# Attention over long keys on one core: VectorE, ScalarE and TensorE programs turned into one-block loops

## The chip, the cores and the metric

The kernel runs on one core of one Trainium2 chip. The metric is the device time of that core in microseconds (us), lower is better.

## The reference

```python
B, H, Sq, Skv, Dh = 8, 16, 16, 2048, 256          # bfloat16 throughout
scale = q.shape[-1] ** -0.5
scores = jnp.einsum('bhqd,bhkd->bhqk', q, k) * scale
attn = softmax(scores, axis=-1)
return jnp.einsum('bhqk,bhkd->bhqd', attn, v)
```

There are 128 heads with 16 queries each. K and V are 128 MB each (in units of 2^20 bytes) and are read once, so about 269 million bytes must come from HBM. Eight heads make a block; there are 16 blocks, each with 8 MB of K and 8 MB of V.

## The kernel before

Each engine has a list of jobs. A job counts up a semaphore when it is done, and later jobs wait for its value. The lists are written out as straight programs, except for TensorE, whose blocks 1 to 14 are one loop.

By a fetch this document means one instruction packet in the trace's DMA records. In the span of the kernel before there are ten: four of 16 KB on queue 8 and six of 8 KB on queue 14. Queue 8's are put down to TensorE. Queue 14's are put down to VectorE, ScalarE and SyncE: with VectorE and ScalarE straight again it carried seven in place of two. By a fetch block we mean the instructions that one such packet holds. How many those are is an estimate: three of queue 14's packets begin after the 57th, 186th and 316th instruction of VectorE in the trace, 129 and 130 apart, so about 130 for 8 KB and 260 for 16 KB. `head_slot` is the program's request at which slot of such a block a loop's first instruction is placed.

## Time and profile before

| what | value |
|---|---|
| time, median | 640.6 us (three runs); 640.75 with those made beside the changed kernel |
| span of the profile | 639.2 us |
| busy: PE, VectorE, ScalarE | 77%, 67%, 16% |
| packet time of all 16 DMA engines, mean of one | 635.1 us |
| granted clock (share of the full TensorE clock) | 0.936 |

First the page of the kernel before: busy time by engine, the 40 slices of the span (a digit is the busy tenth of a slice), and the DMA queues (packets, MB, share of 16 engines).

```profile
span 639.2 us, 4824 instructions
PE 489.1 (77%) x2176; PEld 166.7 (26%) x1680; DVE 427.8 (67%) x372; ACT 99.1 (16%) x208; POOL 4.2 (1%) x7
...
DMA  9999999999999999999999999999999999999996
GB/s 322 428 431 426 432 433 441 435 427 428 421 438 429 431 429 429 437 439 425 437 414 443 431 429 431 425 430 433 437 441 425 432 417 440 429 429 430 421 427 258
...
q1 hardware_dynamic: 13488, 269.51, 98.7%
q10 hardware_dynamic: 2288, 1.03, 0.6%
q8 instruction: 4, 0.07, 0.0%
q14 instruction: 6, 0.05, 0.0%
```

The DMA engines are busy from end to end. The two last lines look like nothing: ten packets of instructions that take 0.0% of the DMA engines.

The chain of waits of the kernel before, in its steady part and at its end (start, length, what):

```profile
429.19 8.90 DVE KB L126 x4
438.09 0.02 issue
438.11 30.14 DMA KN<-in_k_dram
468.25 0.02 issue
468.27 8.90 DVE KB L126 x4
...
556.30 30.15 DMA KN<-in_k_dram
586.45 0.02 issue
...
608.24 28.35 PE O_ps L177 x256
636.59 0.02 issue
636.61 0.48 DVE O_fin L323
```

The first K half of a block lands every 39.08 us, 30 us after its issue. Its own 4 MB take 9.7 us at 431 GB/s; the rest is the queue of loads ahead of it. VectorE and TensorE therefore have slack in the steady part: VectorE waited 139.3 us in all for K loads, TensorE 22.2 us for V loads. At the end TensorE works through 256 matmuls without a gap (28.35 us, with fetches at 617.8 and 631.9 us in it), but its last ones are released by the last loads, as the timeline of the kernel before shows (start, length, engine, line, operation; in brackets the idle time before it and what ended it):

```profile
634.65 1.64 PEld L177 LDWEIGHTS O_ps<-KN,PT 128*128 128x128 bf16 x16 [0.26 <-DMA KN<-in_v_dram]
636.61 0.48 DVE L323 TENSOR_SCALAR O_fin<-O_ps,rab 128x256 bf16<-128x256 f32 x1 [6.66 <-PE O_ps L177]
637.12 0.55 SPq L185 DMA_DIRECT2D out_dram<-O_fin  x1
```

What the views do not print, but the trace holds, are the single completions. Each load counts up its semaphore 16 times; we take each count to be the share of one of the 16 DMA engines. The time from the first to the last of these 16 then says how far the slowest DMA engine is behind the fastest (its backlog). The trace does not say which engine is which, so where the text says that two fetches met the same engine, that is read from how the sizes grow; below are the six last completions of some loads of the kernel before, in us after that load's first one. This is worked out from the trace's semaphore records and is not a view of the profile.

```
load landing at   six last of 16 completions            instruction packets that began shortly before
 12.36            0.19 0.26 0.29 0.30 0.30 0.36
 38.41            0.18 0.26 0.28 0.29 0.36 1.93          36.3 (16 KB)
101.61            0.27 0.28 0.31 0.36 1.09 1.82          95.8 (8 KB)
145.73            0.31 0.31 0.35 0.79 1.14 1.86          140.3 (8 KB)
292.32            0.28 0.28 0.31 0.77 1.83 2.05          289.7 (8 KB)
429.17            0.29 0.30 0.34 1.49 1.87 2.07          419.0 (8 KB)
488.65            0.31 0.33 0.36 1.56 1.92 3.07          486.0 (8 KB)
586.45 (last K)   0.36 0.40 0.95 1.55 1.92 3.10          531.7 (8 KB)
635.93 (last V)   1.52 1.58 1.71 1.92 1.97 3.09          594.8, 617.8, 631.9 (16 KB each)
```

After every instruction packet of this table one of the 16 completions, for us one DMA engine, is 0.5 to 1.6 us further back. Apart from 0.1 us in the next load, it did not catch up by the end; the DMA slices stand at 9 in 39 of 40, so little idle time was left for it. The queue and the counts of instructions issued at those times (57, 186 and 316 of VectorE at 95.8, 289.7 and 486.0) are what we tell by whose fetch it is. By the sizes, VectorE's three fetches add up on one DMA engine: 0.36, 1.09, 2.05, 3.07. A load counts as landed with its slowest engine: the last K's first completion is at 583.34 us and its last at 586.45, and the transposes that wait for it start at 586.47.

### The profile page before, as it was taken

The page shows a single profiled execution, that of the slowest core. Times are in us where ns is not written, and L with a number is a line of the kernel's source. Part 1 is how long each engine was busy: PE and PEld are TensorE (multiplying, and loading weights), DVE is VectorE, ACT ScalarE, POOL GpSimd, SP SyncE. Part 2 cuts the span into 40 slices and gives each one's busy share as a digit, 9 for nine tenths or more (in the row PEclk, how much of TensorE's full clock was granted, in tenths as well). Part 3 has the DMA queues.
Part 4 walks back from the last instruction along what each step waited for, and adds up shares of the span by engine and source line. Part 5 has one row for each costly group of instructions (what it writes and reads, how often), then busy time and mean ns, then how long its engine had stood idle before and what let it go on. Part 6 is the DMA issues. An engine that isn't in the chain of part 4 may idle for free.

```text
span 639.2 us, 4824 instructions
## 1 busy us (share of the span) xinstructions
PE 489.1 (77%) x2176; PEld 166.7 (26%) x1680; DVE 427.8 (67%) x372; ACT 99.1 (16%) x208; POOL 4.2 (1%) x7
## 2 busy tenths in 40 slices
PE   0857879676896768868689686787967878676998
PEld 0111313123131221312214122131311313122287
DVE  4879386693857949387492965938669395693861
ACT  2121112030120301212011120211203012030010
POOL 2000000000000000000000000000000000000000
PEclk9979979799897999899898998997979989899899
DMA  9999999999999999999999999999999999999996
GB/s 322 428 431 426 432 433 441 435 427 428 421 438 429 431 429 429 437 439 425 437 414 443 431 429 431 425 430 433 437 441 425 432 417 440 429 429 430 421 427 258
DMA packets 15786, 270.65 MB, mean 423 GB/s; under 512 B 1824, under 2 KB 4128, under 8 KB 4640
## 3 DMA queue, kind: packets, MB, share of 16 engines
q1 hardware_dynamic: 13488, 269.51, 98.7%
q10 hardware_dynamic: 2288, 1.03, 0.6%
q8 instruction: 4, 0.07, 0.0%
q14 instruction: 6, 0.05, 0.0%
HBM read 269.48 MB, written 1.05 MB: 423 GB/s over the span
## 4 chain that ended last, share of the span: by engine, by line
DMA 67%; DVE 25%; PE 7%; issue 1%; SPq 0%; DVEq 0%
DMA KN<-in_k_dram 67%; DVE KB L126 23%; PE O_ps L177 4%; PE S_ps L143 1%; PE S_ps L131 1%; DVE negm L148 0%; DVE PC L157 0%; SPq L110 0%; DVE PT L163 0%; DVE O_fin L323 0%; DVE O_fin L313 0%; DVE rab L292 0%; DVE rinv L291 0%; DVEq L410 0%; DVE ltot L289 0%
## 5 line engine op out<-in xcount | busy, mean ns | idle before, releaser
L126 DVE STREAM_TRANSPOSE KB<-KN 128x2048 f32<-128x2048 f32 x128 | 284.6, 2281 | 159.7 <-DMA KN<-in_k_dram 139.3
L143 PE MATMUL S_ps<-KB,QW 128*128 128x512 bf16 x528 | 213.1, 413 | 125.2 <-DVE KB L126 125.2
L171 PE MATMUL O_ps<-VB,PT 128*128 128x512 bf16 x896 | 200.7, 386 | 22.2 <-DMA VB<-in_v_dram 22.2
L131 PE MATMUL S_ps<-KB,QW 128*128 128x512 bf16 x496 | 203.9, 411 | 0.0
L143 PEld LDWEIGHTS S_ps<-KB,QW 128*128 128x128 bf16 x528 | 54.0, 103 | 327.7 <-issue 239.4
L171 PEld LDWEIGHTS O_ps<-VB,PT 128*128 128x128 bf16 x896 | 87.9, 99 | 138.0 <-issue 38.6
L119 ACT ACTIVATE QW<-QT 32x128 bf16<-32x128 bf16 x128 | 53.9, 421 | 320.5 <-PE S_ps L131 312.8
L163 DVE COPY PT<-PC 32x1024 bf16<-32x1024 bf16 x128 | 53.3, 416 | 4.3 <-PE O_ps L177 2.6
L157 DVE STREAM_TRANSPOSE PC<-P_sb 128x1024 bf16<-128x1024 bf16 x32 | 37.9, 1223 | 19.8 <-ACT P_sb L152 19.8
L152 ACT ACTIVATE P_sb<-S_ps,negm 128x1024 bf16<-128x1024 f32 x32 | 35.4, 1110 | 36.3 <-DVE negm L148 26.7
L148 DVE TENSOR_REDUCE negm<-S_ps 128x1 f32<-128x2048 f32 x16 | 36.7, 2292 | 4.6 <-PE S_ps L131 4.1
L308 ACT ACTIVATE O_tmp<-O_ps,rab 128x256 f32<-128x256 f32 x15 | 7.1, 474 | 157.9 <-PE O_ps L171 157.1
L177 PE MATMUL O_ps<-KN,PT 128*128 128x256 bf16 x128 | 14.4, 273 | 0.0
L177 PE MATMUL O_ps<-VB,PT 128*128 128x256 bf16 x128 | 14.1, 273 | 0.1
L177 PEld LDWEIGHTS O_ps<-VB,PT 128*128 128x128 bf16 x128 | 12.4, 98 | 2.0 <-DVE PT L163 0.6
L177 PEld LDWEIGHTS O_ps<-KN,PT 128*128 128x128 bf16 x128 | 12.4, 98 | 1.8 <-DMA KN<-in_v_dram 0.3
L323 DVE TENSOR_SCALAR O_fin<-O_ps,rab 128x256 bf16<-128x256 f32 x2 | 1.0, 483 | 11.5 <-PE O_ps L177 11.5
L313 DVE SCALAR_TENSOR_TENSOR O_fin<-O_ps,rab,O_tmp 128x256 bf16<-128x256 f32 x15 | 6.7, 448 | 1.8 <-issue 1.8
L152 ACT ACTIVATION_READ_ACCUMULATOR P_sb<-S_ps,negm 128x1 f32 x32 | 6.3, 196 | 0.0
L113 DVE STREAM_TRANSPOSE QT<-VB 128x2048 f32<-128x2048 f32 x1 | 2.3, 2311 | 5.5 <-DMA VB<-in_q_dram 5.5
L292 DVE TENSOR_SCALAR rab<-mask,rinv 128x2 f32<-128x2 f32 x16 | 3.7, 228 | 0.6
L190 POOL MEMSET PT<- 128x4096 f32 x1 | 3.5, 3512 | 0.0
(11 smaller groups left out, 7.8 us busy)
## 6 DMA issues: line engine op xcount, KB each, us to landing
KN<-in_k_dram SPq DMA_DIRECT2D x28, 4096.0 KB, 30.1
VB<-in_v_dram SPq DMA_DIRECT2D x32, 2048.0 KB, 26.5
VB<-in_v_dram SPq DMA_DIRECT2D x14, 4096.0 KB, 20.0
KN<-in_k_dram SPq DMA_DIRECT2D x8, 2048.0 KB, 15.3
KN<-in_v_dram SPq DMA_DIRECT2D x2, 2048.0 KB, 27.6
KN<-in_v_dram SPq DMA_DIRECT2D x2, 1024.0 KB, 23.1
KN<-in_v_dram SPq DMA_DIRECT2D x3, 512.0 KB, 25.8
VB<-in_q_dram SPq DMA_DIRECT2D x4, 256.0 KB, 4.4
```

The source lines that it names most:

```text
L119: ins = eng.activation(ap_of(dv, dv.offset + 32 * a + e, [[256, 4], [128, 2], [2, 16]]), ap_of(sv, sv.offset + 2 * (2 * g + e), [[64, 4], ...
L126: return eng.transpose(KBf[:, c % R_KB].rearrange("p t i -> p (t i)"), KNf[:, e].rearrange("p t i -> p (t i)")[:, n * c:n * c + n])
L131: return eng.add_instruction(mybir.InstMatmult(start_tensor_calc=start, stop_tensor_calc=stop, ldweights=False, tile_size=(128, 128), tile ...
L143: ins = mm(S_ps[:, 2 * h + c, :], QW[:, e, bp, :], rhs, start=(e == 0 and bp == 0), stop=(e == 1 and bp == 7))
L148: return eng.tensor_reduce(out=negm[:, g:g + 1], in_=S_ps[:].rearrange("p c n -> p (c n)"), axis=AX.X, op=ALU.max, negate=True)
L152: return eng.activation(P_sb[:, 1024 * h:1024 * h + 1024], S_ps[:, 2 * h:2 * h + 2, :].rearrange("p c n -> p (c n)"), ACTF.Exp, bias=negm[ ...
L157: return eng.transpose(PC[:, h].rearrange("p t x -> p (t x)"), P_sb[:, 1024 * h:1024 * h + 1024])
L163: ins = eng.tensor_copy(PT[pr, 32 * h:32 * h + 32, pr], PC[pr, h])
L171: ins = eng.matmul(O_ps[:, 0, :], PT[:, t, :], rhs, start=(t == 0), stop=(t == NT - 1))
L177: ins = eng.matmul(O_ps[:, bank, 0:D], PT[:, t, :], buf[:, t, :], start=(t == 0), stop=(t == NT - 1))
L308: j_ea[g] = J("act", "ea", lambda eng: eng.activation(O_tmp[:], src, ACTF.Copy, scale=rab[:, g, 0:1]), [("pv", g, 1) if g < last - 1 else ...
L313: j_eb[g] = J("dve", "eb", lambda eng: eng.scalar_tensor_tensor(out=O_fin[:, g % 2, :], in0=src, scalar=rab[:, g, 1:2], in1=O_tmp[:], op0= ...
```

## The change

The change is meant to let the programs run without fetches, as TensorE's loop does in the kernel before: it makes 14 turns, and queue 8 has no packet between 36.3 and 594.8 us. Each of the three compute engines gets a loop of one block, placed with `head_slot`. To make all turns alike, it drops the per-block columns of the statistics, uses one exponential for both halves, moves the query scaling behind the exponential, keeps one output buffer, and lets SyncE begin the stores, behind the K loads. A planner removes waits that other waits imply. Its core:

```diff
+PE_SLOT, DVE_SLOT, ACT_SLOT = 8, 144, 80
...
-        O_fin = ec(nc.sbuf_tensor("O_fin", [128, 4, D], BF16))
+        O_fin = ec(nc.sbuf_tensor("O_fin", [128, 3, D], BF16))
...
-        def emit_exp(eng, g, h):
-            return eng.activation(P_sb[:, 1024 * h:1024 * h + 1024],
-                                  S_ps[:, 2 * h:2 * h + 2, :].rearrange("p c n -> p (c n)"), ACTF.Exp,
-                                  bias=negm[:, g:g + 1], scale=1.0, accum_out=lsum[:, g, h:h + 1])
+        def emit_exp(eng):
+            return eng.activation(P_sb[:], S_ps[:].rearrange("p c n -> p (c n)"), ACTF.Exp,
+                                  bias=negm[:], scale=1.0, accum_out=lsum[:])
...
             for u in (2 * g, 2 * g + 1):
                 k_load(u)
+            if g >= 3:
+                store("sp", g - 3)
...
+        for g in range(last):
             softmax_act(g)
+            qwb(g + 1)
+            if g:
+                evac_a(g - 1)
...
+        turns = {"dve": [order["dve"][dve_head + n * x:dve_head + n * x + n] for x in range(G - 2)],
+                 "pe": [order["pe"][0:4]] + [order["pe"][6 * x - 2:6 * x + 4] for x in range(1, last)],
+                 "act": [order["act"][1:3]] + [order["act"][3 * x:3 * x + 3] for x in range(1, last)]}
...
+            with nc.Fori(0, 4 * len(ts) - 3, 4, engines=engines, head_slot={eng.engine: slot}) as it:
+                ...
+                part(full[:len(first)])
+                if len(first) < len(full):                      # first turn of TensorE and ScalarE is shorter
+                    nc.br_lt(it, 4, on_true=after, on_false=rest, engines=engines)
...
-    emit_pe(nc.tensor)                                          # head of block 0 straight, loop at slot 0
+    emit_stream(nc.scalar, "act", ACT_SLOT)
+    emit_stream(nc.vector, "dve", DVE_SLOT)
+    emit_stream(nc.tensor, "pe", PE_SLOT)                       # block 0 is now the loop's first turn
```

## The prediction

> **What bounds the kernel now.** The transfers. The page's slices show the DMA engines at 9 in 39 of 40 slices, at about 430 GB/s. The packet records add up, per engine on the mean of 16, to 631.2 us for loads and 3.6 for stores: 634.8 of a span of 639.2. PE is busy 77%, VectorE 67%, ScalarE 16%. In the steady part the chain of waits repeats every 39.07 us: 30.13 waiting for a K load, 8.90 of four K transposes. A K load lands 30 us after its issue, and only 9.7 us of that are its own 4 MB at 431 GB/s: 20 us of other loads stand ahead, so compute may be several us later without the queue running dry. The bytes (269.5 MB read, 1.05 written) stay, so most of the 640.6 us cannot move.

> **What can move: instruction fetches.** [...] ten instruction packets in the span, at 36, 96, 140, 290, 419, 486, 532, 595, 618 and 632 us. A load packet beside one takes 0.37 to 0.66 us longer. The delay stays on that engine: from the first to the last of the 16 completions of a load are 0.36 us until 32 us, 1.8 after the first fetch, 2.1 after 290, 3.1 from 486 to the end. A load has landed only when its slowest engine has. The last V part ends at 632.84 on the first engine, 635.93 on the last; 0.7 us later the last matmul ends, then a scaling (0.48) and the last store (2.0).

> **What the change does.**
> - VectorE's program shrinks from 424 instructions to 112, ScalarE's from 244 to 49: their fetches vanish or fall to one each. PE's head goes into its loop: the fetch at 36 us goes. PE's straight tail keeps three late fetches, about 1.6 us each on different engines. End spread 3.1 to about 2.0: minus 1.1 us, on the critical path.
> - One exponential of 2048 instead of two of 1.11 + 0.20: about 2.2 us; the first P transpose waits 0.9 longer. VectorE then idles 10 us for K, and in the last block waits 2.56 us for PE: 0.
> - Query scaling moves behind the exponential (8 x 0.42 us plus registers), over 5 us before the next K: 0.
> - Stores go to the load queue behind K, same 512-byte packets (27 ns each). The single output buffer waits for a store that lands with K, 8.9 us before it is needed: 0.
> - Loop registers and branches: under 1 us per block, in idle time. The extra small copy: 0 to 0.2.

> **Sum.** 640.6 - 1.3 = 639.3 us, 637.6 to 640.7 eight times in ten. Faster by over 2%: 0.01; within 2%: 0.97; slower: 0.02.

> **What would show it.** Instruction packets in the span: ten to three to six. Spread of a K load's completions at 550 us: 0.4 to 1 instead of 3.1. The same 39.05 us period, GB/s unchanged in the middle slices.

> **What would make it wrong.** A loop that misses its loaded block on each turn; stores that leave bubbles between loads (period over 39.1 us); register waits or branches that cost several us on VectorE before the last block; PE's serial tail (28.35 us of matmuls without a gap from 608.24) hiding the earlier landing.

The traces bear out its figure for the registers and the branch of a loop (under 1 us per block): from the start of the first such instruction at the head of a turn to the end of the last, TensorE's loop in the kernel before takes 0.40 to 0.49 us, and in the kernel after TensorE's takes 0.41 to 0.50, VectorE's 0.32 to 0.68 and ScalarE's 0.27 to 0.28; ScalarE's query scaling adds eight register instructions of 46 ns.

## The result

The changed kernel took 640.76 us (median of six runs, 640.60 to 640.97) and the kernel before 640.75 us (six runs, 640.50 to 640.93): no change. The ratio is 1.0, 95% interval 0.9988 to 1.0013. The ratios are not quite the ratios of the medians quoted.

The page of the kernel after, the lines that answer to those above:

```profile
span 639.1 us, 5084 instructions
PE 487.3 (76%) x2176; PEld 166.1 (26%) x1680; DVE 428.2 (67%) x371; ACT 93.8 (15%) x176; POOL 4.2 (1%) x7
...
DMA  9999999999999999999999999999999999999996
...
q1 hardware_dynamic: 15360, 270.36, 99.2%
q10 hardware_dynamic: 416, 0.18, 0.1%
q8 instruction: 4, 0.07, 0.0%
q14 instruction: 2, 0.02, 0.0%
```

The loops did what they were meant to do for VectorE and ScalarE: queue 14 carries two packets in place of six. TensorE's queue 8 still carries four. All but the last stores moved from queue 10 to queue 1.

The chain of waits of the kernel after, at its end:

```profile
555.60 30.09 DMA KN<-in_k_dram
585.69 0.03 issue
...
594.70 0.33 SPq L230
595.03 0.04 issue
595.07 30.42 DMA KN<-in_v_dram
625.49 0.14 issue
625.63 10.80 PE O_ps L178 x96
```

Before, the last K landed at 586.45 and TensorE then ran 256 matmuls in one piece; now the last K lands at 585.69, 0.76 us earlier, but TensorE stops at 625.49 to wait for a V part and does its last 96 matmuls behind it. The timeline of the kernel after says how the 0.76 us were lost:

```profile
607.40 14.15 PE L178 MATMUL O_ps<-VB,PT 128*128 128x256 bf16 x128 [0.35 <-DVE PT L164]
...
625.63 10.79 PE L178 MATMUL O_ps<-KN,PT 128*128 128x256 bf16 x96 [0.59 <-DMA KN<-in_v_dram]
...
634.49 1.64 PEld L178 LDWEIGHTS O_ps<-KN,PT 128*128 128x128 bf16 x16 [0.25 <-DMA KN<-in_v_dram]
636.53 0.48 DVE L325 TENSOR_SCALAR O_fin<-O_ps,rab 128x256 bf16<-128x256 f32 x1 [6.66 <-PE O_ps L178]
```

TensorE starts its last matmuls 0.84 us earlier than before (607.40 for 608.24), but the scaling behind them starts only 0.08 us earlier. Most of the loss is the wait of 0.59 us for a V part at 625.63, which the kernel before does not have; the short wait near the end (0.25 us) was there before (0.26). The completions, as above:

```
load landing at   six last of 16 completions            instruction packets that began shortly before
  9.62 (query)    0.43 0.46 0.58 0.60 1.40 2.60          3.6 (16 KB)
 14.21            0.31 0.36 0.41 0.42 1.26 2.24
 87.40            0.38 0.42 0.43 1.13 1.28 2.26          76.3 (8 KB)
458.69            0.52 0.55 1.20 1.29 1.32 2.34          452.7 (8 KB)
585.69 (last K)   0.61 0.64 1.32 1.36 1.41 2.45
596.05            0.63 0.67 1.33 1.36 2.45 3.08          593.9 (16 KB)
635.77 (last V)   1.26 1.31 1.69 2.00 2.43 2.85          617.0, 631.7 (16 KB each)
```

The fetch that I expected to vanish with TensorE's head did not vanish. It moved from 36.3 us to 3.6 us, among the first loads, where the slowest engine fell back by 2.2 us and a second one by 1.3. And the late fetch at 593.9 fell, as the sizes suggest, on an engine that was already 1.4 us behind. The slowest engine ended 2.85 us behind the first, before it was 3.09. The prediction had named a spread of 0.4 to 1 us for a K load at 550 us as a sign; it is 2.40 us (landing at 556.30), so this sign failed too, long before the end.

### The profile page after: what moved, and what is told of

It reads as the page before. It is cut to its first block, busy times and chain, and to the rows that moved or that the text cites. A ratio compares the mean times of both kernels' runs of the same rounds, so it can differ in the third digit from the quotient of the medians.

```text
span 639.1 us, 5084 instructions
## 1 busy us (share of the span) xinstructions
PE 487.3 (76%) x2176; PEld 166.1 (26%) x1680; DVE 428.2 (67%) x371; ACT 93.8 (15%) x176; POOL 4.2 (1%) x7
## 3 DMA queue, kind: packets, MB, share of 16 engines
HBM read 269.48 MB, written 1.05 MB: 423 GB/s over the span
## 4 chain that ended last, share of the span: by engine, by line
DMA 72%; DVE 17%; issue 5%; PE 4%; ACT 0%; SPq 0%; DVEq 0%; ACTq 0%
DMA KN<-in_k_dram 67%; DVE KB L128 17%; DMA KN<-in_v_dram 5%; PE O_ps L178 2%; PE S_ps L145 1%; PE S_ps L133 1%; DVE negm L150 0%; ACT QW L122 0%; SPq L110 0%; DVE O_fin L325 0%; SPq L230 0%; DVEq L480 0%; ACT P_sb L154 0%; ACTq L122 0%; ACTq L483 0%
## 5 line engine op out<-in xcount | busy, mean ns | idle before, releaser
L172 PEld LDWEIGHTS O_ps<-VB,PT 128*128 128x128 bf16 x896 | 87.5, 99 | 136.4 <-issue 35.7
L154 ACT ACTIVATE P_sb<-S_ps,negm 128x2048 bf16<-128x2048 f32 x16 | 31.5, 1968 | 399.9 <-DVE negm L150 399.9
L122 ACT ACTIVATE QW<-QT 32x128 bf16 (+1 forms) x128 | 54.0, 422 | 11.4 <-DVE QT L113 10.0
L300 DVE COPY rab<-rab 128x2 f32<-128x2 f32 x15 | 2.5, 167 | 1.3
```

The lines of the kernel that those rows point to most:

```text
L122: ins = eng.activation(ap_of(dv, dv.offset + 32 * a + e, [[256, 4], [128, 2], [2, 16]]), src.rearrange("p (s b) t -> p b t s", b=4), ACTF. ...
L154: return eng.activation(P_sb[:], S_ps[:].rearrange("p c n -> p (c n)"), ACTF.Exp, bias=negm[:], scale=1.0, accum_out=lsum[:])
L172: ins = eng.matmul(O_ps[:, 0, :], PT[:, t, :], rhs, start=(t == 0), stop=(t == NT - 1))
```

## The experiments

The theory: **the end is set by the DMA engine with the most backlog, and the backlog is the sum of the instruction fetches that fell on it.** The rivals: the gain was eaten by work that the change adds on the compute engines (loop registers and branches, the later transpose of P, the exponentials), or by the stores in the load queue. The first four runs shared a chip and the runs of the kernel before on it (640.71 us, nine runs), the last four another (640.65 us, nine runs).

### TensorE's head straight again

```diff
-PE_SLOT, DVE_SLOT, ACT_SLOT = 8, 144, 80
+PE_SLOT, DVE_SLOT, ACT_SLOT = 0, 144, 80
-                 "pe": [order["pe"][0:4]] + [order["pe"][6 * x - 2:6 * x + 4] for x in range(1, last)],
+                 "pe": [order["pe"][6 * x - 2:6 * x + 4] for x in range(1, last)],
```

> The kernel after, with TensorE's first block again as straight code ahead of its loop. Theory (the slowest DMA engine's backlog sets the end): the fetch that fell at 3.6 us goes back to about 36 us; the spread of a K load's 16 completions near 300 us is 1.8 to 1.9 us and not 2.27; the last V part lands about 2.0 us after its first engine and not 2.85; the time falls by 0.5 to 1.0 us against both kernels. Rival (the gain is eaten by work that the loops add on VectorE, ScalarE and TensorE): TensorE's head changes nothing there, so the time stays within 0.2 us of the kernel after.

Measured: 639.96 us against 640.71, a gain of 0.75 us; ratio 0.9991 (0.9977 to 1.0004). The first fetch is at 35.7 us again. The completions spread by 0.50 us at 12 us and by 2.0 at the last K; the last V lands at 635.11, 1.92 us after its first engine. In the timeline of this kernel:

```profile
606.75 14.15 PE L178 MATMUL O_ps<-VB,PT 128*128 128x256 bf16 x128 [0.36 <-DVE PT L164]
...
633.87 1.64 PEld L178 LDWEIGHTS O_ps<-KN,PT 128*128 128x128 bf16 x16 [0.33 <-DMA KN<-in_v_dram]
635.90 0.48 DVE L325 TENSOR_SCALAR O_fin<-O_ps,rab 128x256 bf16<-128x256 f32 x1 [6.74 <-PE O_ps L178]
```

The last matmuls, released by the last loads, and the last scaling come 0.6 us earlier than in the kernel after. Nothing changed on VectorE and ScalarE, so their added work was not what held the kernel after back. The gain is close to the noise in the ratio's interval, but all five runs (639.81 to 640.28) lie below all nine of before (640.36 to 640.86), and the trace has it in the same place. The same kernel with harmless writes added (below) repeats it on the other chip: all five runs (639.77 to 639.98) below all nine of before (640.40 to 640.83).

### VectorE and ScalarE straight again

```diff
+        turns = {"pe": turns["pe"]}
```

> The kernel after, with VectorE and ScalarE as straight programs again; only TensorE loops. Theory: their fetches come back (nine or ten instruction packets in the span), the completion spread grows in steps and is 3.1 us or more at the end; the time is 0 to 0.6 us longer than after. Rival (loop registers and branches cost the gain): at least 0.5 us shorter than after, as the loops' overhead is gone.

Measured: 642.23 us, 1.5 us longer than before and than the changed kernel; ratio to before 1.0025 (1.0012 to 1.0039). Queue 14 carries seven packets. With TensorE's four that makes eleven, where nine or ten were expected. The direction is the theory's; the size was underestimated. In this form VectorE's straight program is longer than that of the kernel before (519 instructions in its trace for 424), so it makes four fetches, at 92, 248, 404 and 562 us, and they take the slowest engine to 4.30 us behind the first. The last V lands at 637.10. So the loops do pay: they save 1.5 us against the same work unrolled.

### Two exponentials again

```diff
-        def emit_exp(eng):
-            return eng.activation(P_sb[:], S_ps[:].rearrange("p c n -> p (c n)"), ACTF.Exp,
-                                  bias=negm[:], scale=1.0, accum_out=lsum[:])
+        def emit_exp(eng, h):
+            return eng.activation(P_sb[:, 1024 * h:1024 * h + 1024],
+                                  S_ps[:, 2 * h:2 * h + 2, :].rearrange("p c n -> p (c n)"), ACTF.Exp,
+                                  bias=negm[:], scale=1.0, accum_out=lsum[:, h:h + 1])
... (each P transpose waits for its own half; the two sums are added)
```

> The kernel after, with two exponentials of 1024 columns and the sum of their two sums again. Theory: VectorE's wait for the exponential lies in its idle time, so the time stays within 0.2 us of the kernel after. Rival (the later P transpose eats the gain): 0.5 us or more shorter than after.

Measured: 640.99 us for the kernel after's 640.76, 0.23 us longer, where at most 0.2 was expected and the rival asked for 0.5 shorter; the last V lands at 635.80 for 635.77. The one exponential took no time that these runs can tell. The rival falls.

### TensorE's loop at slot 64

```diff
-PE_SLOT, DVE_SLOT, ACT_SLOT = 8, 144, 80
+PE_SLOT, DVE_SLOT, ACT_SLOT = 64, 144, 80
```

> The kernel after, with TensorE's loop moved from slot 8 to slot 64 of a fetch block[...]. A dose test: if crossing a block starts a fetch, there are about two TensorE fetches per turn, some 30 instruction packets of 16 KB. Theory: each costs one DMA engine about 1.5 us for good; if they fall on all 16 engines in turn the time grows by 2 to 4 us, if on a few, by over 10 us, and the completion spread shows which. Rival (fetches are hidden and cost no transfer time): the time stays within 0.3 us, at most TensorE shows idle time in front of its matmuls.

Measured: 640.67 us. As a dose test this failed: there were not 30 TensorE fetches but four, at 3.1, 38.3, 613.5 and 629.0 us. A turn has 231 TensorE instructions in the trace; with the estimate of about 260 for a packet of 16 KB, a loop from slot 64 ends at about slot 295 and so lies across two blocks. That is the estimate; where the boundary is, was not shown. (The 2 to 4 us and over 10 us of the expectation are estimates too: 30 fetches of 1.5 us are 45 us, 2.8 for each of 16 engines, 11 for each of four.) The DMA view of this kernel from 40 to 580 us, more than 13 turns, has no packet of TensorE's queue 8:

```profile
q1 hardware_dynamic: 11796, 232.77, 100.5%
q14 instruction: 2, 0.02, 0.0%
```

So these turns ran without a TensorE fetch. The fetch at 3.1 us left two engines 1.57 and 1.04 us behind here (load landing at 13.64), less than in the kernel after; the one at 38.3 took the slowest to 2.49 us (load landing at 43.92). The placement of this loop thus added no fetch per turn (four TensorE fetches in the span, as in the kernel after), but it moved the few there are (613.5 and 629.0 us for 617.0 and 631.7). The time follows the slowest engine as the theory says: it ends 2.53 us behind, and the last V lands at 635.67.

### All three programs as far straight as before, the rest of the change kept

This is the TensorE edit and the VectorE and ScalarE edit together.

> The kernel after with TensorE's head out of the loop and VectorE and ScalarE straight: all three engines fetch as before, the rest of the change (one exponential, moved query scaling, one-column statistics, single output buffer, stores begun by SyncE) stays. Theory (only the fetches move the time): three VectorE fetches stack on one DMA engine, the completion spread at the end is 3.0 to 3.3 us (perhaps 4 if a fourth VectorE fetch falls before the last load, as in the run with both straight), and the time is that of before within 0.3 us, or 1.0 us longer in the second case; 0.7 to 2.0 us longer than with the loops and the head out. Rival (stores or the exponential cost or gain time of their own): the end is not where the slowest completion plus 3.3 us puts it.

Measured: 641.92 us, 1.27 us longer than before; ratio 1.0021 (1.0007 to 1.0035). The fourth VectorE fetch falls at 561.7 us, so the second case came: the slowest engine is 4.00 us behind and the last V lands at 637.09. The 1.3 us are a little more than the 1.0 expected. The end comes 3.35 us after the last completion (3.26 to 3.38 in all ten traces), and the first engine's last share is done at 633.10 for 632.84, so at most a few tenths are left for the stores or the exponential to explain. With TensorE's head in the loop the same kernel ended at 637.10: while VectorE's fetches make the slowest engine, it did not matter where TensorE's first one fell.

### More VectorE instructions, straight and in the loop

Both kernels get 32 one-column writes per block, at the head of blocks 2 to 15, where VectorE waits 8 to 10 us for K. The first is the kernel before (straight), the second the kernel with TensorE's head out (loop).

```diff
+        def pad():
+            def emit(eng):
+                for x in range(32):
+                    ins = eng.memset(padt[:, x:x + 1], 0.0)
+                return ins
+            J("dve", "pad", emit)
...
+            if g >= 2:
+                pad()
```

> The kernel before, with 32 one-column writes of a scratch tile added to VectorE at the head of each block from the third on, where it waits 8 to 10 us for K: 448 more instructions in its straight program. Theory: about 3.5 more VectorE fetches, each 0.9 us of backlog on the same DMA engine; the completion spread ends at 6.0 to 6.7 us and the time grows by 3.0 to 3.6 us, to about 644. Rival (the fetches are harmless, and added VectorE work lies in idle time): within 0.3 us of before.

> The control: the same 32 writes per block at the same place, inside VectorE's loop of the kernel with TensorE's head out. Same added work, 32 more instructions in the program. Theory: no added fetch but perhaps one, no growth of the spread: within 0.3 us of the kernel with the head out (639.96). Rival (the added work itself costs time): 2 us or more longer, as in the run with the straight program.

Measured: the straight one takes 644.38 us, 3.73 us more than before; ratio 1.0059 (1.0045 to 1.0072). The loop takes 639.88, which against its rounds' 640.65 is a gain of 0.77 as without the writes (0.75). The same added work costs 3.7 us in one form and nothing in the other. (The two kernels differ in the rest of the change too; each is compared with the same kernel without the writes.) In the straight form the slowest engine's backlog climbs in steps of about 1 us after each VectorE fetch:

```
load landing at   six last of 16 completions            VectorE fetch before
 77.42            0.35 0.39 0.40 0.51 1.12 1.93           72.7
155.75            0.43 0.44 0.45 0.74 1.95 2.15          150.7
254.34            0.40 0.44 0.45 0.76 1.97 3.18          252.8
333.46            0.41 0.46 0.46 0.80 2.00 4.19          332.0
417.49            0.40 0.45 0.47 0.81 2.01 5.20          416.0
511.21            0.40 0.46 0.48 1.53 1.99 6.04          504.9
590.30 (last K)   0.49 0.53 1.00 1.60 1.97 6.98          584.0
639.77 (last V)   0.95 1.47 1.69 1.88 1.97 6.95
```

Seven fetches for three before, so four were added where I had worked out 3.5 (448 instructions, at the 129 or 130 between VectorE's fetches in the kernel before), and 1.0 rather than 0.9 us each: 6.95 us in place of the 6.0 to 6.7 expected, and 3.73 in place of 3.0 to 3.6. The first engine still has its share of the last V at 632.83, as before (632.84). The chain of waits of this kernel shows the same wait for the last K with a later landing, 590.30 for 586.45:

```profile
559.24 31.06 DMA KN<-in_k_dram
590.30 0.02 issue
590.33 8.90 DVE KB L127 x4
```

### Stores begun by SyncE, alone

```diff
             for u in (2 * g, 2 * g + 1):
                 k_load(u)
+            if g >= 3:
+                store(g - 3, "sp")
... (ScalarE begins the last two alone; still two output buffers)
```

> The kernel before, with its stores begun by SyncE behind the K loads, except the last two; nothing else changed. Theory: same bytes and packets in another queue: the 39.07 us period and the time stay within 0.3 us, apart from ScalarE fetches that come at other times. Rival (stores in the load queue leave bubbles, which hid a gain of the change): period over 39.1 us and 1 us or more longer.

Measured: 640.94 us for 640.65, ratio 1.0004 (0.999 to 1.0018). The slowest engine ends 3.23 us behind instead of 3.09, and the last V lands at 636.26. The stores are not where a gain was lost. Whether the 0.3 us come from the stores or from fetches at other times is not settled. Its trace does not name the DMA engines that carry the stores.

### All ten traces together

| kernel | time, us | last V: first engine | last V: slowest engine | behind | span | span less slowest |
|---|---|---|---|---|---|---|
| loop, head out, writes added | 639.88 | 633.02 | 635.07 | 2.05 | 638.4 | 3.36 |
| loop, head out | 639.96 | 633.19 | 635.11 | 1.92 | 638.5 | 3.38 |
| loop at slot 64 | 640.67 | 633.14 | 635.67 | 2.53 | 639.0 | 3.35 |
| after | 640.76 | 632.92 | 635.77 | 2.85 | 639.1 | 3.34 |
| two exponentials | 640.99 | 632.99 | 635.80 | 2.81 | 639.1 | 3.33 |
| before | 640.75 | 632.84 | 635.93 | 3.09 | 639.2 | 3.26 |
| before, stores by SyncE | 640.94 | 633.03 | 636.26 | 3.23 | 639.5 | 3.28 |
| straight, head out | 641.92 | 633.10 | 637.09 | 4.00 | 640.4 | 3.35 |
| straight | 642.23 | 632.80 | 637.10 | 4.30 | 640.4 | 3.34 |
| before, writes added | 644.38 | 632.83 | 639.77 | 6.95 | 643.0 | 3.26 |

The mean packet time of a DMA engine is 635.0 to 635.5 us in all ten: the work is the same, and only its distribution differs. The first engine is done at 633.0 within 0.2 us in all of them. The slowest one differs by 4.7 us, and the end follows it at 3.26 to 3.38 us. That distance is 3.26 to 3.28 in the three forms of the kernel before and 3.33 to 3.38 in the seven with the rest of the change, so the rest of the change costs about 0.1 us at the end.

## Why the prediction was wrong

**The mechanism held.** The prediction said that the transfers bound the kernel, that instruction fetches throw single DMA engines back for good, and that a load has landed only when its slowest engine has. What it got wrong is where TensorE's fetches fall and what they meet there. The padded pair shows this as directly as these runs can: equal added work, with fetches 3.7 us, without them nothing.

**The term that failed is the first one of the sum: "End spread 3.1 to about 2.0: minus 1.1 us, on the critical path".** It was 2.85, and the slowest engine's last completion moved by 0.16 us (635.93 to 635.77). Two steps under it were wrong.

1. *"PE's head goes into its loop: the fetch at 36 us goes."* It moved to 3.6 us. In the kernel before, TensorE's matmuls of block 0 end at 36.1 us, the loop's first branch is at 32.7 and the fetch begins at 36.3; in the kernel after, the loop comes first, its first branch is at 0.9 and the fetch begins at 3.6. In both the fetch follows the loop's first branch, by 3.6 and 2.7 us. So I read, from these two traces alone, that it belongs to the entry into the loop, and that the change only made TensorE enter earlier. Among the first loads the fetch cost more: the slowest engine was 2.24 us behind at 14 us and a second one 1.26, where after the fetch at 36.3 us it was one engine, 1.93 and then 1.8 us behind. Putting the head back gave 0.75 us and a spread of 1.92: close to the 1.1 and 2.0 that I had claimed for the change itself.
2. *"Three late fetches, about 1.6 us each on different engines."* I counted them as if each met an engine without backlog, as the one at 594.8 had done before (0.40 to 1.97). In the kernel after, the one at 593.9 met, as the sizes suggest, an engine 1.41 us behind and took it to 2.86. The second engine of the fetch at 3.6 us stood at 1.26 us from then on (1.27 in the load landing at 77.69) and is probably this one, so both steps would have one cause; with the head out the fetch at 593.9 left its engine 1.97 behind, and the end spread was 1.92. The 0.76 us that the last K had gained were given back there, mostly in TensorE's wait of 0.59 us for V.

**What was right.** VectorE's and ScalarE's fetches fell from six packets to two (with SyncE's among them: 79 instructions of SyncE come before the packet at 531.7 us in the kernel before and before the one at 452.7 in the kernel after), and that alone is worth 1.5 us against the same program unrolled. Instruction packets in the span are six, foretold were three to six; but TensorE still makes four where three were foretold, so this sign could not tell that the step had failed. The steady period is 39.08 us before (429.17 to 468.25) and after (429.32 to 468.40). TensorE's serial tail, which the prediction named as a risk, did not hide a gain: in the kernel after it waits 0.59 us for V. The single exponential costs nothing that shows (640.76 us, with two 640.99). The stores, tried alone, leave the time within 0.3 us (640.94 for 640.65). The query scaling, the extra copy and the loop registers were not tried one by one; that together they cost no more than about 0.1 us at the end is argued from the last column of the table.

**The range.** Its upper end, 640.7, lay within the scatter of the kernel before (640.50 to 640.93). "Nothing happens" deserved to be inside it.

**What stays open.** Why the fetch at 3.6 us throws two engines back (1.3 and 2.2 us), when the record has one packet (some packets may be missing from the records), and why it cost less, 1.57 and 1.04 us, with the loop at slot 64. And which DMA engine serves which fetch: by the sizes VectorE's fetches fell on one and the same engine all the time (with the added writes 1.12, 2.15, 3.18, 4.19, 5.20, 6.04, 6.98 us after its seven fetches), TensorE's four in the kernel before on different ones (1.5 to 2.0 us each at the end), but the trace does not name them.

## What to carry to other kernels

When the DMA engines are busy from end to end, the mean can hide the finish (here 635.0 to 635.5 us in all ten traces, while the slowest engine ended between 635.07 and 639.77): compare the first and the last of the 16 completions of a load, since small packets can add up on one engine, as by the sizes VectorE's fetches did here at 0.0% of the traffic (3.07 us after three, 6.98 after seven). Shorten a straight program for its fetches only after finding whose fetches make the slowest engine; here, while VectorE's made it, moving TensorE's head changed the last landing by 0.01 us (637.09 and 637.10). And ask where a fetch goes that a rearrangement "removes": keeping the first block straight and looping the rest was the better mix (639.96 us, 0.1% below both kernels, near the limit of what five runs can tell).
